# Two neighbouring loads swapped in the first q phase, and a group of small matmuls moved three column tiles later

## The chip, the cores and the metric

The kernel runs on one core of one Trainium2 chip. The metric is the time of one execution on the device in microseconds (us), lower is better. Each kernel is run several times, alternating with the kernel before on the same chip; "span" is the time from the first to the last instruction in the profiled execution, which is about 1.8 us less than the device time of that execution.

## The reference

One transformer block: layer norm with a conditioned scale and shift ("adaLN"), linear attention, and a gated feed-forward part.

```python
def reference(A_x, A_wqkv, A_wo, B_x, B_w_gate, B_w_up, B_w_down, c, w_mod):
    x = A_x                                         # (1, 2048, 1024), bf16
    mod = (_silu(c) @ w_mod).reshape(c.shape[0], 6, 1, -1)
    sa, ca, ga, sb, cb, gb = ...                    # shift, scale, gate; 1024 each   [cut]
    h = _layernorm(x, axis=-1) * (1 + ca) + sa
    x = x + ga * _A_ref(h, A_wqkv, A_wo)            # q, k, v = h @ wqkv ...
    h = _layernorm(x, axis=-1) * (1 + cb) + sb
    x = x + gb * _B_ref(h, B_w_gate, B_w_up, B_w_down)
    return x
```

The change touches only the first step: the scale `ca` (columns 1024-2047 of `w_mod`) and the q part of `h @ wqkv` for the first 512 of 2048 rows. That is the first 30 us of 830.

## The kernel before

The first phase is a race between the load queue and TensorE. All loads of the phase are put on one queue, in this order:

```python
        ca_load(0)          # w_mod columns of the scale, 0-511, 1 MB     -> WCA
        wq_load(0, 2)       # q weights, k-tiles 0 and 1, 512 KB          -> WQK
        ca_load(1)          # scale columns 512-1023, 1 MB
        wq_load(2, 2)       # q weights, k-tiles 2 and 3, 512 KB
        wq_load(4, 2)
        sa_load(1)          # shift columns 512-1023, 1 MB                -> WSA
        wq_load(6)
        wq_load(7)
        sa_load(0)          # shift columns 0-511, 1 MB
        # ... x tiles of the next chunk, k weights ...   [cut]
```

`mod_sc` multiplies those columns by silu(c), one output column per matmul; `q_part` adds some k-tiles to the q product of one column tile `nt`; there are seven column tiles in flight, one PSUM bank each.

```python
        def mod_sc(w, c0, ms):                       # 8 matmuls of ONE column for each m
            for m in ms:
                for kt in range(NDT):
                    P.pe("matmul", out=PS[:, 0, c0 + m:c0 + m + 1], lhsT=w[:, kt, m * 128:(m + 1) * 128],
                         rhs=SILUC[:, kt:kt + 1], ...)           # [cut]

        def q_part(nt, bank, dts):                   # one matmul of 512 columns for each dt
            for dt in dts:
                P.pe("matmul", out=PS[:, bank, :], lhsT=WQK[:, dt, nt * 128:(nt + 1) * 128],
                     rhs=HT[:, 0, dt, :], start=(dt == 0), stop=(dt == 7))

        def q_phase_chunk0(side):
            # ... k-tiles 0 and 1 of the seven column tiles: 14 matmuls   [cut]
            mod_sc(WCA, 8, range(4, 8))              # 32 one-column products: needs ca_load(1)
            fin_ca(4, 4)
            for dt in (4, 5):
                h0_scale_only(dt)                    # VectorE makes k-tiles 4, 5 of the activations
            for nt in range(7):
                q_part(nt, qb[nt], (2, 3))           # 14 matmuls: needs wq_load(2, 2)
            act_stats(4)
            for nt in range(7):
                if nt == 4:
                    mod_sc(WSA, 0, range(6, 8))      # 16 one-column products: needs sa_load(1)
                    # ...   [cut]
                q_part(nt, qb[nt], (4, 5))
            # ... k-tiles 6 and 7, mixed with the other shift columns   [cut]
```

Dependencies are found by the program itself: each instruction waits on semaphores for the last writer or readers of what it touches.

## Time and profile before

| | before |
|---|---|
| device time, median of 3 | 831.19 us (831.15 to 832.09) |
| span of the profiled execution | 829.4 us |
| TensorE matmul busy | 824.0 us, 99% |
| weight-load busy | 378.4 us, 46% |
| VectorE / ScalarE busy | 38% / 24% |

The chain of work that ended last, in order of time (start us, length us, what), is one TensorE piece from 8.76 us to the end. Ahead of it stand the load of the third x tile and the operations of VectorE (DVE) and ScalarE (ACT) that make this tile ready:

```profile
...
1.71 4.21 DMA xres<-in_A_x_dram
...
5.94 1.29 DVE stats L176 x2
...
7.47 1.23 ACT xres L176
8.71 0.05 issue
8.76 818.08 PE ps L176 x4069
826.83 0.02 issue
826.86 0.29 DVE xres L176
```

The waits of TensorE (waited for: us in total, times, longest us) name no weight and no scale column:

```profile
...
PE ps L176 <- DMA cs<-in_c_dram: 2.2, 1, 2.2
PE ps L176 <- ACT xres L176: 0.4, 1, 0.4
PE ps L176 <- DVE e L176: 0.2, 1, 0.2
```

The timeline of TensorE in the first q phase (start us, us to the end of the group, operation, count, and in brackets the idle time before it). `siluc,wca` are scale-column products, `ht,wqk` are q products, `siluc,wsa` are shift-column products:

```profile
...
12.43 3.18 PE L176 MATMUL ps<-ht,wqk 128*128 128x512 bf16 x14
15.45 0.94 PE L176 MATMUL ps<-siluc,wca 128*128 128x1 bf16 x32
16.25 4.91 PE L176 MATMUL ps<-ht,wqk 128*128 128x512 bf16 x22
21.00 0.54 PE L176 MATMUL ps<-siluc,wsa 128*128 128x1 bf16 x16
...
```

Read the *starts*, not the busy times. 22 q products from 16.25 to 21.00 are (21.00 - 16.25) / 22 = 0.216 us each. The Trainium skill ("TensorE: Matmul & The Clock Gate", "Wait — 56ns, not 53.3ns?") gives 215.7 ns from start to start for 512 columns on a warm array; this trace agrees, so no wait hides among them. One record, however, lasts 0.38 us (mean of the q-product group), longer than the step to the next one. So a wait shorter than about 0.16 us leaves no idle time at all in this view, and a longer one looks 0.16 us shorter than it is. The view also leaves out idle times under 0.15 us, so that waits up to about 0.3 us can be missing from it.

The same stretch for weight loads shows when each load is first *wanted*: 0.21 us ahead of the matmul for the column products, which follow q products (15.24 and 15.45, 20.79 and 21.00), and 0.02 us ahead for the q products, which follow column products (16.23 and 16.25):

```profile
...
15.24 1.06 PEld L176 LDWEIGHTS ps<-siluc,wca 128*128 128x128 bf16 x32
16.23 4.44 PEld L176 LDWEIGHTS ps<-ht,wqk 128*128 128x128 bf16 x22
20.79 0.66 PEld L176 LDWEIGHTS ps<-siluc,wsa 128*128 128x128 bf16 x16
...
```

And these loads *landed* (all 16 shares of each) at 14.80 (scale columns 512-1023), 16.17 (q weights 2-3) and 20.46 (shift columns 512-1023); the shift columns 0-511 landed at 24.83 and were wanted at 25.11. The margins are 0.44, 0.06, 0.33 and 0.28 us, counted to the weight load. (No view shows the shares; they are read from the semaphore updates in the kept traces.)

### The profile page before, as it was taken

Reading aid. Unit: us, or ns where it says so; the run is one execution under the profiler, and the core shown is the slowest. Engines: PE = TensorE matmul, PEld = TensorE weight load, DVE = VectorE, ACT = ScalarE, POOL = GpSimd, SP = SyncE. Lnnn points to the kernel's source line nnn. Section 1 sums busy time; section 2 is a strip of 40 time slices with the busy share of each in tenths; the row PEclk is TensorE's granted clock in tenths of the full one; section 3 lists DMA queues with packets and bytes.
Section 4 is the critical chain, followed back from the end, with each engine's and each line's share of the span. In section 5 each row is a group of like instructions: output and inputs, shape, how many; then the busy total and the mean of one; then the engine's idle time right before and its main releaser. Section 6 shows DMA issues by size and latency. Waiting matters only on the chain.

```text
span 829.4 us, 10017 instructions
## 1 busy us (share of the span) xinstructions
PE 824.0 (99%) x4083; PEld 378.4 (46%) x4083; DVE 312.0 (38%) x665; ACT 197.6 (24%) x336; POOL 39.8 (5%) x57
## 2 busy tenths in 40 slices
PE   8999999999999999999999999999999999999998
PEld 4544444454444444444444444444444444444444
DVE  5797986756955521121221111122111111221111
ACT  4757641323242111011111101111110111111011
POOL 1010000000130000030000003000000300000000
PEclk9999999999999999999999999999999999999999
DMA  9969655928397996700455570045557004553000
GB/s 320 288 151 229 149 159 172 202 102 304 60 258 225 259 267 174 192 25 14 128 150 155 150 188 28 15 126 153 153 153 187 26 18 125 154 151 86 0 26 26
DMA packets 199245, 119.28 MB, mean 144 GB/s; under 512 B 57880, under 2 KB 182944, under 8 KB 199200
## 3 DMA queue, kind: packets, MB, share of 16 engines
q1 hardware_dynamic: 199184, 118.65, 52.7%
q8 instruction: 32, 0.52, 0.3%
q14 instruction: 13, 0.11, 0.0%
q10 hardware_dynamic: 16, 0.00, 0.0%
HBM read 100.67 MB, written 4.33 MB: 127 GB/s over the span
## 4 chain that ended last, share of the span: by engine, by line
PE 99%; DMA 1%; DVE 0%; ACT 0%; SPq 0%; issue 0%
PE ps L176 99%; DMA xres<-in_A_x_dram 1%; DVE stats L176 0%; ACT xres L176 0%; SPq L176 0%; DVE xres L176 0%; DVE mv L176 0%; DVE nmr L176 0%
## 5 line engine op out<-in xcount | busy, mean ns | idle before, releaser
L176 PE MATMUL ps<-h2t,gug 128*128 128x512 bf16 x896 | 211.7, 379 | 0.0
L176 PE MATMUL ps<-h2t,guu 128*128 128x512 bf16 x896 | 211.7, 379 | 0.0
L176 DVE TENSOR_TENSOR at<-sg,ps 128x512 bf16<-128x512 bf16 x112 | 77.1, 688 | 282.7 <-PE ps L176 281.1
L176 ACT ACTIVATE sg<-ps 128x512 bf16<-128x512 f32 x112 | 66.9, 597 | 309.7 <-PE ps L176 309.7
L176 PEld LDWEIGHTS ps<-h2t,guu 128*128 128x128 bf16 x896 | 87.5, 98 | 105.8
L176 PEld LDWEIGHTS ps<-h2t,gug 128*128 128x128 bf16 x896 | 87.4, 98 | 105.7
L176 PE MATMUL ps<-wd_a,at 128*128 128x512 bf16 (+1 forms) x512 | 112.4, 378 | 0.0
L176 PE MATMUL ps<-ht,wqk 128*128 128x512 bf16 x512 | 111.7, 379 | 0.0
L176 PE MATMUL ps<-wd_b,at 128*128 128x512 bf16 (+1 forms) x384 | 85.0, 378 | 0.0
L176 PEld LDWEIGHTS ps<-wd_a,at 128*128 128x128 bf16 x512 | 50.0, 98 | 59.8
L176 DVE TENSOR_TENSOR ut<-att,gb_b 128x512 bf16<-128x512 bf16 (+1 forms) x32 | 13.8, 430 | 167.5 <-ACT att L176 167.5
L176 PEld LDWEIGHTS ps<-ht,wqk 128*128 128x128 bf16 x512 | 49.4, 98 | 58.8
L176 ACT ACTIVATE att<-ps 128x512 bf16<-128x512 f32 (+1 forms) x32 | 17.4, 591 | 182.1 <-PE ps L176 182.1
L176 PEld LDWEIGHTS ps<-wd_b,at 128*128 128x128 bf16 x384 | 37.5, 98 | 44.7
L176 PE MATMUL ps<-pk,xres 128*128 128x512 bf16 x256 | 56.5, 379 | 0.0
L176 PE MATMUL ps<-mw,pqt 128*128 128x512 bf16 x256 | 56.3, 379 | 0.0
L176 POOL TENSOR_SCALAR h2t<-h2t,modcol 128x512 bf16<-128x512 bf16 x32 | 26.4, 841 | 383.0 <-DMA h2t<-xn 383.0
L176 ACT ACTIVATE e<-ps 128x512 bf16<-128x512 f32 x56 | 33.1, 603 | 31.7 <-PE ps L176 20.5
L176 PEld LDWEIGHTS ps<-mw,pqt 128*128 128x128 bf16 x256 | 24.8, 98 | 30.3 <-DVE xres L176 0.4
L176 PEld LDWEIGHTS ps<-pk,xres 128*128 128x128 bf16 x256 | 24.8, 98 | 30.0 <-issue 0.4
L176 ACT ACTIVATE junk<-xres 128x1024 bf16<-128x1024 bf16 x24 | 25.4, 1058 | 35.1 <-DVE xres L176 34.9
L176 DVE SCALAR_TENSOR_TENSOR xres<-ps,xres 128x512 bf16<-128x512 f32 x32 | 21.4, 689 | 12.3 <-PE ps L176 11.7
(107 smaller groups left out, 346.0 us busy)
## 6 DMA issues: line engine op xcount, KB each, us to landing
gug<-in_B_w_gate_dram SPq DMA_DIRECT2D x56, 512.0 KB, 3.9
guu<-in_B_w_up_dram SPq DMA_DIRECT2D x56, 512.0 KB, 5.2
xres<-in_A_x_dram SPq DMA_DIRECT2D x20, 256.0 KB, 7.8
rb<-recip_den SPq DMA_DIRECT2D x8, 512.0 KB, 11.5
stgx<-in_w_mod_dram SPq DMA_DIRECT2D x2, 2048.0 KB, 7.8
wd_a<-in_B_w_down_dram SPq DMA_DIRECT2D x4, 1024.0 KB, 7.8
out_dram<-xres SPq DMA_DIRECT2D x31, 128.0 KB, 1.7
xres<-in_A_x_dram SPq DMA_DIRECT2D x3, 1024.0 KB, 14.0
```

Of the source, the lines that this page charges most:

```text
L176: return getattr(e, method)(**kw)
```

## The change

Intent: the q weights of k-tiles 2 and 3 are the load with the least time in hand. They change places with the larger load ahead of them, and to make up for that, the products of the load that is now later go three column tiles (six matmuls) later. No work is added or removed.

```diff
         ca_load(0)
         wq_load(0, 2)
+        wq_load(2, 2)
         ca_load(1)
-        wq_load(2, 2)
         wq_load(4, 2)
@@
-            mod_sc(WCA, 8, range(4, 8))
-            fin_ca(4, 4)
-            for dt in (4, 5):
-                h0_scale_only(dt)
             for nt in range(7):
+                if nt == 3:
+                    mod_sc(WCA, 8, range(4, 8))
+                    fin_ca(4, 4)
+                    for dt in (4, 5):
+                        h0_scale_only(dt)
                 q_part(nt, qb[nt], (2, 3))
```

## The prediction

> **What bounds the kernel.** TensorE, without a pause. The chain of waits that ended last is one unbroken TensorE piece from 8.76 us to 826.83 us (818.08 of 829.4 us). The list of TensorE's waits holds three, 2.8 us in all, every one before 8.8 us; none is for a q weight or a scale column. In the timeline of the first q phase, 22 matmuls of 512 columns start at 16.25 and the next group at 21.00: 0.216 us each. The Trainium skill ("TensorE: Matmul & The Clock Gate", "Wait — 56ns, not 53.3ns?") gives 215.7 ns from start to start on a warm array; the trace agrees, so no stall hides inside the "busy" time. The 32 scale-column products take 15.45 to 16.25, 0.80 us.
>
> **What the change does.** It adds and removes no work; it moves two things.
> 1. Load order. The 1 MB of scale columns 512-1023 and the 512 KB of q weights 2-3 swap. The DMA engines are saturated here (about 360 GB/s from 5 to 30 us in the windows). Landings, from issue plus time to landing: scale columns 14.80, q weights 16.17. First uses, from the weight-load rows of the timeline: 15.24 and 16.23; margins 0.44 and only 0.06 us. The Trainium skill ("DMA: Bandwidth & Descriptors", "Queues, rings and completion order") says that each DMA engine takes descriptors in ring order, and the landings here follow the issue order. So after the swap q weights 2-3 should land at about 13.2 (the first q-weight load's 11.80 plus 1.37, the step between two such loads, 16.17 to 17.55), the scale columns at about 16.2, later loads as before.
> 2. Product order. The k-tile 2-3 products of three column tiles (6 x 0.216 = 1.29 us) go ahead of the scale-column products. They start at 15.24 with 2.0 us in hand; the scale columns are then needed at 16.53, margin about 0.36 us. VectorE makes k-tiles 4-5 ready 1.04 us after the column products end (before: 16.26 to 17.30), thus at about 18.6; their first use stays at about 19.2. No new wait.
>
> **On the critical path.** All the matmuls are, but their sum does not change and no wait before them exists to be removed. The tightest of these margins grows from 0.06 to about 0.3 us (shift columns: landed 20.46, used 20.79, unchanged). That is insurance: it pays only in executions where a load is late. The profiled run (831.22 us) equals the median (831.19), so unprofiled runs hardly stall either. I take 0.05 us for occasional lateness.
>
> **Predicted: 831.1 us, 8 in 10 from 830.5 to 831.9.** Faster by over 2%: 0.005; within 2%: 0.99; slower by over 2%: 0.005.
>
> **What would show it.** Right: one TensorE piece of about 818 us from about 8.8; no wait on a weight or scale load; six q products from about 15.45, the 32 column products at about 16.74; q weights 2-3 landing near 13.2, scale columns near 16.2; everything from 21.0 at its old time. Wrong: a start-to-start over 0.216 us at the scale-column products (columns late) or at the first k-tile 4 product near 19.3 (VectorE late); or a gain over 0.3 us, which would mean stalls in the unprofiled runs of before.
>
> **What would make it wrong.** The 0.06 us margin fails often in unprofiled runs or on another chip, so the swap gains some tenths; or the scale columns land over 0.36 us later than computed; or the start (8.76 us) or the array's warm-up differs between runs by more than these tenths (832.09 was seen among three).

## More of the kernel before

All runs quoted here are at a granted clock of 1.0. The runs of experiments 1 and 2 come from one chip (5), those of 3 and 4 from a second (15), those of 5 from a third (8); for the first result no chip is on record. Profiles of different experiments can thus differ by the chip, too.

## The result

| | before | after |
|---|---|---|
| device time, median (lowest to highest) | 831.21 us (830.95 to 832.09, 6 runs) | 830.94 us (830.53 to 831.58, 6 runs) |
| span of the profiled execution | 829.4 us | 829.4 us |
| ratio after/before | | 0.9996, 95% interval 0.9983 to 1.0009: same |

A ratio here is the mean time of one kernel's fast runs over the mean of the other's in the same rounds, so it is not quite the ratio of the medians in the table.

The total looks like nothing happened. The profile after does not. The chain now has a detour through a load:

```profile
...
7.79 13.09 DMA wsa<-in_w_mod_dram
20.88 0.05 issue
20.93 805.88 PE ps L176 x3932
826.81 0.02 issue
826.83 0.29 DVE xres L176
```

The waits of TensorE have a new entry:

```profile
...
PE ps L176 <- DMA cs<-in_c_dram: 2.2, 1, 2.2
PE ps L176 <- ACT xres L176: 0.9, 1, 0.9
PE ps L176 <- DMA wsa<-in_w_mod_dram: 0.2, 1, 0.2
PE ps L176 <- DVE e L176: 0.2, 1, 0.2
```

The timeline of TensorE in the same phase:

```profile
...
11.97 4.48 PE L176 MATMUL ps<-ht,wqk 128*128 128x512 bf16 x20
16.29 0.94 PE L176 MATMUL ps<-siluc,wca 128*128 128x1 bf16 x32
17.09 3.61 PE L176 MATMUL ps<-ht,wqk 128*128 128x512 bf16 x16
20.93 0.55 PE L176 MATMUL ps<-siluc,wsa 128*128 128x1 bf16 x16 [0.23 <-DMA wsa<-in_w_mod_dram]
...
```

Its weight loads:

```profile
...
16.07 1.06 PEld L176 LDWEIGHTS ps<-siluc,wca 128*128 128x128 bf16 x32
17.07 3.14 PEld L176 LDWEIGHTS ps<-ht,wqk 128*128 128x128 bf16 x16
20.93 0.47 PEld L176 LDWEIGHTS ps<-siluc,wsa 128*128 128x128 bf16 x16 [0.71 <-DMA wsa<-in_w_mod_dram]
...
```

Three things are to be read here.

First, the move itself is as designed: 14 + 6 = 20 q products, then the 32 column products, then 16 q products. The columns are done at 17.09, VectorE has k-tiles 4 and 5 ready at 18.15, 1.06 us later, and their first use follows at 17.09 + 8 x 0.216 = 18.82 without a wait.

Second, one and the same wait at the shift columns is told three ways: 0.23 us in the TensorE row, 0.71 us in the weight-load row, and by the starts 20.93 - 17.09 - 16 x 0.216 = 0.39 us. Only the last is what it cost. The first is too small because a matmul's modelled end lies after the next one's usual start: the Trainium skill ("Perfetto Trace Analysis", "Tensor Engine Instruction (MATMUL, LD_WEIGHTS)") says that the end is estimated, and records of 0.38 us at steps of 0.216 us agree. The second is too large because the weight row is idle about 0.12 us before each load anyway, and the wanted load runs ahead of the matmul: it came 0.59 us late, the matmul 0.39 us. So the margins at column products (0.44, 0.33 and 0.28 us) understate by 0.15 to 0.2 us how late a load may come before it costs anything; the 0.06 us at q weights 2-3 does not.

Third, the chain's shares changed a lot (TensorE 99% before; 97% after, with DMA 2% and the issuing queue 1%) because of a 0.39 us wait. A chain is followed back through what released a wait, so a wait of any length turns it off TensorE, here for the whole 13.09 us in which that load stood in the queue. The shares don't price the wait.

TensorE started the q products 0.46 us earlier than in the profile before (11.97 against 12.43) and lost 0.39 us of it at the shift columns. The change did not touch that start: the loads and operations that TensorE needs up to 12 us are the same ones, in the same order, in both kernels. So is the 0.46 us luck, and the 0.39 us a price of the change? The first has an answer in the kept traces. In the profile before, the third x tile landed at 5.92 us and TensorE's first transpose of the phase started at 8.76; in the profile after, 5.45 and 8.29. In eleven of the twelve profiles of this document the second follows the first by 2.84 us (3.07 in late_room). That tile is issued ahead of everything that the change moves, and its landing varies from 5.06 to 6.13 us; why, the traces don't tell. On the second: the shift columns keep their place in the queue and in TensorE's order, 36 q products and 32 column products after q start (8.57 us, 12.43 to 21.00 in the profile before). With this start and this landing the kernel before would have waited as long. Whether the swap itself can delay that landing takes experiments.

### The profile page after: what moved, and what is told of

Read it like the earlier page. It is cut to its first block, busy times and chain, and to the rows that moved or that the text cites. A ratio compares the mean times of both kernels' runs of the same rounds, so it can differ in the third digit from the quotient of the medians.

```text
span 829.4 us, 10017 instructions
## 1 busy us (share of the span) xinstructions
PE 823.2 (99%) x4083; PEld 378.8 (46%) x4083; DVE 312.6 (38%) x665; ACT 197.5 (24%) x336; POOL 39.9 (5%) x57
## 4 chain that ended last, share of the span: by engine, by line
PE 97%; DMA 2%; SPq 1%; issue 0%; DVE 0%
PE ps L176 97%; DMA wsa<-in_w_mod_dram 2%; SPq L176 1%; DVE xres L176 0%
## 6 DMA issues: line engine op xcount, KB each, us to landing
xres<-in_A_x_dram SPq DMA_DIRECT2D x3, 1024.0 KB, 14.1
```

## The experiments

Two theories were put up.

- **Theory S (sum).** The time is TensorE's start plus a fixed sum of matmuls plus whatever waits remain on loads. A wait is paid once, in full.
- **Theory F (floor of the loads).** In the first phase TensorE runs into the load stream. What it wins in front it gives back at the next load, so waits trade against each other and the end does not move.

Twelve profiles are read in the same way. *q start* is the start of the first q product (of the filler, where there is one); *waits* are the sum, after that point, of the excess of start-to-start over 0.216 us per q product (and 0.80 us for 32 column products) at those places where a load is waited for; *rest* is span minus q start minus waits, and minus 0.86 us of filler where there is one. Waits ahead of q start, on x tiles and on the first scale columns, are inside q start (in after_again 0.59 us at the latter). A wait of 0.03 us in after and in late_after, at shift columns 0-511, is left in the rest.

| profile | q start | waits on loads, us (where) | span | rest |
|---|---|---|---|---|
| before | 12.43 | 0 | 829.44 | 817.01 |
| after | 11.97 | 0.39 (shift 512-1023) | 829.42 | 817.06 |
| before_again | 12.65 | 0 | 829.62 | 816.97 |
| after_again | 12.83 | 0 | 829.81 | 816.98 |
| loads_only | 12.23 | 0.46 (scale 512-1023) | 829.67 | 816.98 |
| products_only | 12.17 | 0.31 (q weights 2-3) | 829.55 | 817.07 |
| pad4_before | 12.24 | 0 | 830.11 | 817.01 |
| pad4_after | 12.55 | 0 | 830.39 | 816.98 |
| late_before | 12.09 | 0.85 (scale) + 0.54 (q 2-3) | 830.47 | 816.99 |
| late_after | 12.30 | 1.02 (scale) + 0.13 (shift) | 830.50 | 817.05 |
| room | 12.18 | 0 | 829.18 | 817.00 |
| late_room | 11.92 | 0.26 (scale) + 0.53 + 0.46 (shift) | 830.15 | 816.98 |

### 1. The kernels again: `before_again` and `after_again`

No edit; the same two kernels on another occasion, five runs each.

> The kernel before, once more, unchanged: the noise floor and a second profile. Theory S (TensorE's sum is the floor; the waits of the first phase are zero or a few tenths): ratio 1.000 within 0.0005, chain of TensorE without a wait from about 8.8 us. Theory F (in the first phase TensorE runs into the DMA stream, so waits there come and go with the landing of the slowest share of a load): this profile shows another pattern, a wait of 0.1 to 0.9 us at q weights 2-3 or at the shift columns, and TensorE's start of the q phase and that wait trade against each other, so that the shift-column products still start at 20.9 to 21.5.

> The changed kernel, unchanged: a second profile. Theory S: ratio to the kernel before 0.9995 to 1.0000. Theory F: also near 1, because the wait at the shift columns (0.23 us in the first profile of the changed kernel) takes what the front won; the shift-column products start at 20.7 to 21.3, right at the landing of their load, in this profile too.

Measured: before_again 831.40 us median (830.89 to 831.71), ratio 1.0001 (0.9988 to 1.0013). After_again 831.57 us (831.20 to 832.32), ratio 1.0005 (0.9992 to 1.0017), against 830.99 us for the kernel before. So the changed kernel was 0.27 us ahead in the first series and 0.58 us behind in this one, by medians, both inside the intervals: no difference. (Theory S had expected a ratio of 0.9995 to 1.0000 for after_again; 1.0005 is above that, inside the noise.)

The profile of after_again has no wait at the shift columns. It has one that the change can't have made, at the scale columns 0-511, the first load of the phase:

```profile
...
11.12 0.55 PE L176 MATMUL ps<-siluc,wca 128*128 128x1 bf16 x16 [0.44 <-DMA wca<-in_w_mod_dram]
...
12.83 4.48 PE L176 MATMUL ps<-ht,wqk 128*128 128x512 bf16 x20
17.14 0.94 PE L176 MATMUL ps<-siluc,wca 128*128 128x1 bf16 x32
17.95 3.61 PE L176 MATMUL ps<-ht,wqk 128*128 128x512 bf16 x16
21.40 0.54 PE L176 MATMUL ps<-siluc,wsa 128*128 128x1 bf16 x16
...
```

Eight transposes start at 10.08, and where no load is waited for the products after them follow 0.45 us later; here they start at 11.12 instead of 10.53, 0.59 us late, and from there everything is late by that much. The margins that the prediction had read from a single profile are thus not constants. Here are the landings of two loads, by shares (a load is done when the last of its 16 shares has landed):

```
us: first / eighth / last of 16 shares      q weights 2-3            shift columns 512-1023
before                                      14.22 / 14.47 / 16.17    18.52 / 18.77 / 20.46
before_again                                13.93 / 14.24 / 15.76    18.26 / 18.54 / 20.20
after                                       11.15 / 11.57 / 11.97    18.43 / 18.86 / 20.88
after_again                                 11.11 / 11.71 / 13.79    18.66 / 19.05 / 21.13
```

With the same load order, the first half of the shares lands within about 0.5 us from one execution to the next; the last share lags by 0.8 to 2.7 us behind the first, and by different amounts. Neither the chip nor the loads ahead explain this: for q weights 0-1, up to which all kernels have the same queue, the lag was 1.83, 2.72, 1.61 and 1.44 us in the four profiles of experiments 1 and 2, all from one chip. Within one execution, however, the lag is not drawn anew at each load. In these four profiles and in before and after it stays the same within 0.1 us over the five loads that follow the x tiles, and can take another value, steady again, from shift columns 512-1023 on: 1.9 and 1.9 us in before, 0.8 and 2.45 us in after. So the wait in after came about by an x tile that was early by 0.46 us together with a lag that grew by 1.6 us. The swap moves the first share of q weights 2-3 by about 2.9 us (14.1 to 11.1), which is the other load's share of the stream; what the last share does on top is not explained by these runs. Theory F's expectation for this pair (a wait at one of the two loads in before_again, shift columns starting right at their landing in after_again) failed: no wait, and starts at 21.21 with a landing at 20.20 and at 21.40 with one at 21.13. (The range given for the first start, 20.9 to 21.5, did hold, but at TensorE's own pace.) The second was close: the first weight load followed the landing by 0.05 us (21.18), but the products kept their pace.

### 2. Half of the change at a time: `loads_only` and `products_only`

```diff
 loads_only: the loads swapped, the products where they were
-        ca_load(1)
         wq_load(2, 2)
+        ca_load(1)

 products_only: the products moved (as in the change), the loads in the old order
```

> Only the load order is swapped; the column products stay ahead of all q products of k-tiles 2-3. Scale columns 512-1023 land at 15.0 to 16.2 and are wanted at 14.8 to 15.24. Theory S: a wait of 0.2 to 0.9 us at the column products and the same amount more time (ratio 1.0003 to 1.001). Theory F: a wait there, too, but the wait at the shift columns shrinks by as much, so the total is within 0.2 us of the kernel before.

> Only the products are moved; loads as in the kernel before. The first q products of k-tile 2 want their weights at 14.8 to 15.24, and these land at 15.0 to 16.2. Theory S: a wait of 0.2 to 0.9 us at the first k-tile-2 product, and as much more time. Theory F: the wait is there but is paid back at the shift columns; total within 0.2 us of the kernel before.

Measured: loads_only 831.47 us (831.12 to 831.98), ratio 1.0003 (0.999 to 1.0016); products_only 831.33 us (830.79 to 831.79), ratio 1.0002 (0.9989 to 1.0016). The device times can't tell either from the kernel before. The profiles can. In loads_only TensorE comes to the scale columns too early:

```profile
...
12.23 3.18 PE L176 MATMUL ps<-ht,wqk 128*128 128x512 bf16 x14
15.71 0.95 PE L176 MATMUL ps<-siluc,wca 128*128 128x1 bf16 x32 [0.30 <-DMA wca<-in_w_mod_dram]
16.52 4.91 PE L176 MATMUL ps<-ht,wqk 128*128 128x512 bf16 x22
21.27 0.54 PE L176 MATMUL ps<-siluc,wsa 128*128 128x1 bf16 x16
...
```

15.71 - 12.23 - 14 x 0.216 = 0.46 us of wait, and none after it: it is carried to the end. In products_only TensorE comes to q weights 2-3 too early, and here the TensorE row shows no idle time at all:

```profile
...
12.17 4.79 PE L176 MATMUL ps<-ht,wqk 128*128 128x512 bf16 x20
16.80 0.94 PE L176 MATMUL ps<-siluc,wca 128*128 128x1 bf16 x32
17.60 3.61 PE L176 MATMUL ps<-ht,wqk 128*128 128x512 bf16 x16
21.05 0.54 PE L176 MATMUL ps<-siluc,wsa 128*128 128x1 bf16 x16
...
```

The 20 q products take 16.80 - 12.17 = 4.63 us instead of 20 x 0.216 = 4.32; one step, at the first product of k-tile 2, is 0.31 us too long. In the list of waits of the weight loads it does appear:

```profile
...
PEld ps L176 <- DMA wqk<-in_A_wqkv_dram: 0.6, 1, 0.6
...
```

So each half by itself opens a wait of 0.3 to 0.5 us where its load is the later of two, in one profile each, and the two halves of the change belong together. Both waits were paid, as theory S says, but q started 0.2 to 0.3 us earlier than in the profile before, so the spans hardly differ.

### 3. Filler ahead of the phase: `pad4_before` and `pad4_after`

```diff
             fin_ca(2, 2)
             for dt in (2, 3):
                 h0_first(dt, "dve")
+            warm(4, bank=3)        # four idle matmuls of 512 columns: 0.86 us
             for nts, dts in (...):
```

If the loads set the pace, TensorE has time to spare in front of them, and a filler is free; if TensorE's sum sets it, the filler costs its length.

> The kernel before with four idle 512-column matmuls (0.86 us) put ahead of the first q product; nothing else. Theory S (TensorE's sum plus whatever waits remain): both profiles of the kernel before had no wait on a load, so all of it is paid: +0.86 us, ratio about 1.0010, and no wait on a load in the profile. Theory F (the loads pace the first phase): most of it is absorbed in front of the loads, under +0.4 us, ratio under 1.0005.

> The changed kernel with the same four matmuls. Theory S: +0.86 us less the waits that this hides (0 to 0.39 us at the shift columns in the two profiles so far), so +0.5 to +0.86 us, ratio 1.0006 to 1.0010; no wait at the shift columns. Theory F: under +0.4 us.

Measured: pad4_before 831.83 us (831.75 to 832.41), ratio 1.0007 (0.9994 to 1.0021); pad4_after 832.20 us (831.95 to 833.18), ratio 1.0012 (1.0000 to 1.0025); the kernel before 831.28 us. The intervals are wide: +0.55 and +0.92 us by medians, between theory F's limit of +0.4 and the full 0.86 plus noise. The profiles settle it. Neither shows a wait on a load after the filler, and with 0.86 us taken off both have the same rest as the others, 817.01 and 816.98. All of the filler is in the span (pad4_after's ratio, 1.0012, even lies above the 1.0006 to 1.0010 that theory S gave, inside the noise). With loads on time, TensorE's sum is what counts.

### 4. Late on purpose: `late_before` and `late_after`

The swap is insurance, so it should be looked at where it has to pay. Two tiles of x (512 KB) are loaded ahead of the disputed pair instead of after the phase; all later loads of the phase move back by that.

```diff
         wq_load(0, 2)
+        for j in range(2):
+            P.dma("x1_%d" % j, XRES[:, 4 + j, :], xv[:, 4 + j, :])
         ca_load(1)              # late_after: wq_load(2, 2) first, products three tiles later
         wq_load(2, 2)
 ...
         sa_load(0)
-        for j in range(2):
-            P.dma("x1_%d" % j, XRES[:, 4 + j, :], xv[:, 4 + j, :])
```

> Lateness on purpose: two x tiles (512 KB, 1.37 us of the load stream) go ahead of the scale columns and q weights 2-3, which thus land 1.37 us later, and all loads after them up to the shift columns of tiles 0-511; order and products of the kernel before. Theory S with margins of 0.44 and 0.06 to 0.69 us: waits of 0.7 to 0.95 us at the column products and 0 to 0.4 us at the q products after them, 0.7 to 1.3 us in sum, and as much more time (ratio 1.0008 to 1.0016).

> The same lateness in the changed kernel. No wait at q weights 2-3 (2 us in hand); 0.3 to 1.0 us at the column products; then at the shift columns (margin about 0.3 us before, load 1.37 us later) the rest up to about 1.0 us. Sum 0.6 to 1.1 us; so of the insurance that the change buys no more than about 0.3 us shows, because the next margin, which it did not touch, is the limit. Ratio 1.0006 to 1.0014, not clear of the kernel above.

Measured: late_before 832.64 us (831.83 to 833.00), ratio 1.0014 (1.0001 to 1.0026); late_after 832.38 us (831.66 to 832.83), ratio 1.0012 (0.9999 to 1.0025). The order of the two is as expected, but the runs overlap. In late_before both disputed loads are waited for:

```profile
...
12.09 3.18 PE L176 MATMUL ps<-ht,wqk 128*128 128x512 bf16 x14
15.96 0.95 PE L176 MATMUL ps<-siluc,wca 128*128 128x1 bf16 x32 [0.69 <-DMA wca<-in_w_mod_dram]
17.30 4.92 PE L176 MATMUL ps<-ht,wqk 128*128 128x512 bf16 x22 [0.39 <-DMA wqk<-in_A_wqkv_dram]
22.05 0.54 PE L176 MATMUL ps<-siluc,wsa 128*128 128x1 bf16 x16
...
```

In late_after the wait at q weights 2-3 is gone and two others stand in its place, a larger one at the scale columns and a small one (0.13 us, shown by the step to 22.03 alone) at the shift columns:

```profile
...
17.64 0.95 PE L176 MATMUL ps<-siluc,wca 128*128 128x1 bf16 x32 [0.86 <-DMA wca<-in_w_mod_dram]
18.45 3.61 PE L176 MATMUL ps<-ht,wqk 128*128 128x512 bf16 x16
22.03 0.55 PE L176 MATMUL ps<-siluc,wsa 128*128 128x1 bf16 x16
...
```

Waits: 0.85 + 0.54 = 1.39 us against 1.02 + 0.13 = 1.15 us, so 0.24 us less with the change, both sums a little above what was expected (0.7 to 1.3 and 0.6 to 1.1 us). But the q phase happened to start 0.21 us later, which shortens the waits by as much, and the shift-column products start at 22.05 and 22.03, the same. Taken by itself this is what theory F says.

It is not a fair pair, though, because the load streams of the two executions differ. The later load of the disputed pair landed at 17.25 us in late_before (q weights) and at 17.59 in late_after (scale columns), the shift columns at 21.66 and 21.99: 0.34 and 0.33 us later with the change. At each of these waits TensorE went on 0.05 us after the landing. An estimate from these numbers puts late_after on the landings of late_before: scale-column products at 17.30, shift columns wanted at 17.30 + 0.80 + 16 x 0.216 = 21.56, started at 21.71 because their load landed at 21.66. That is 0.34 us ahead of 22.05, so the swap would have paid about 0.3 us, and would have been stopped by the next load in the queue, as was expected. One pair of profiles doesn't show it, and the device times (832.64 and 832.38 us) overlap.

With the loads put back by 1.37 us of the stream, an earlier start of the q phase would only have lengthened the first wait in both kernels. In late_after the insurance ends at the next load in the queue, which the change left as it was.

### 5. More room at two loads: `room` and `late_room`

If the next margin is the limit, widening it too should show. On top of the change, the scale-column products go four tiles late instead of three, and the shift-column products for k-tiles 6-7 one tile later.

```diff
-                if nt == 3:
+                if nt == 4:
                     mod_sc(WCA, 8, range(4, 8))
 ...
-                if nt == 4:
+                if nt == 5:
                     mod_sc(WSA, 0, range(6, 8))
```

> The changed kernel with both margins widened: the scale-column products four column tiles late instead of three, and the shift-column products for k-tiles 6-7 one column tile later (0.43 us each). Theory S: no wait on scale columns 512-1023 or shift columns in the profile unless a load is 0.7 us late; the time is that of both kernels, ratio 0.999 to 1.0005, since there is hardly a wait to remove (0 to 0.4 us per profile so far). q start plus waits on loads plus about 817.0 us gives the span again. A wait of VectorE's making at the first k-tile-4 or k-tile-6 product would show as a matmul step over 0.216 us there; expected none (0.25 and 0.15 us in hand).

> The same widened margins under the lateness of 512 KB. Theory S: the waits fall by 0.43 us against the kernel with the three-tile delay and the same lateness (1.15 us in its profile): 0.3 to 0.8 us in sum, ratio 1.0004 to 1.001. If the loads paced the phase instead (theory F), the sum of q start and waits would stay at 13.4 to 13.5 us, as in the two late kernels; theory S wants about 13.0.

Measured: room 831.28 us (830.95 to 832.06), ratio 1.0004 (0.9990 to 1.0017), no wait on any load in the profile, as expected. Late_room 832.47 us (831.95 to 832.94), ratio 1.0016 (1.0003 to 1.0028): no gain over late_after in device time. Its span is 0.3 us shorter than those of the two late kernels, but the profiled run was also the fastest of its five. Its waits were expected to fall to 0.3 to 0.8 us in sum. They are 0.26 + 0.53 + 0.46 = 1.25 us. The first did fall (1.02 to 0.26), and then the shift columns were waited for twice:

```profile
...
21.71 0.55 PE L176 MATMUL ps<-siluc,wsa 128*128 128x1 bf16 x16 [0.35 <-DMA wsa<-in_w_mod_dram]
...
24.32 1.46 PE L176 MATMUL ps<-ht,wqk 128*128 128x512 bf16 x6
26.07 0.95 PE L176 MATMUL ps<-siluc,wsa 128*128 128x1 bf16 x32 [0.30 <-DMA wsa<-in_w_mod_dram]
```

The second of these, at 26.07, is the *last* large load of the phase (shift columns 0-511, landed 26.03), whose products had not been given more room. q start plus waits is 13.17 us, where the two late kernels have 13.48 and 13.45, theory S wanted 13.0 and theory F 13.4 to 13.5. Half a miss: the widened margins passed the lateness on to the load behind, as in experiment 4. (In these two profiles one matmul record in about fifty is missing, so q start is read from the weight-load rows there, and a missing record is counted as a step.)

No version beats both kernels by anything that these runs can show.

## Why the prediction was right

It was right in what decides: 831.1 us was predicted, 830.94 us measured, in a range of 830.5 to 831.9. That the number came within 0.2 us is partly luck: the same kernel had a median of 831.57 us on the next occasion. What the runs support is that there was nothing to gain.

- *TensorE bounds the kernel, and the change does not alter its sum.* Shown. Twelve profiles give a rest of 816.97 to 817.07 us once q start and waits are taken off, over all the orders of the phase that were tried.
- *No wait to remove.* Shown for q weights 2-3: two profiles of the kernel before have none there, and the q products run at 0.216 us. The products_only kernel, with the old load order, shows that a wait does come up at just this load as soon as its products are wanted earlier.
- *The two halves compensate.* Shown, with one profile of each half: each alone opens a wait (0.46 and 0.31 us), both together none at either load.
- *VectorE is ready in time.* Shown: 1.06 us from the last column product, use 0.67 us after that, no long step.
- *Insurance of at most the difference to the next margin.* Not shown. Under deliberate lateness the waits fell by 0.24 us, but 0.21 us of that is the later q start; TensorE reached the shift columns at the same time, and the device times overlap. On equal landings an estimate (experiment 4) gives 0.34 us, near the predicted difference between margins of 0.06 and 0.3 us. A gain in an execution that is late by chance was not seen.

Three steps of it were wrong in size or stated too firmly.

- *"q weights 2-3 should land at about 13.2 [...], the scale columns at about 16.2".* They landed at 11.97 and 14.96 in one profile, and at 13.79 and 16.80 in the other. The step that was added, 1.37 us from one such load to the next, held (1.36 and 1.35 us). What failed was its base, the landing of q weights 0-1 at 11.80 us in one profile: it was 10.61 and 12.43 us in the two others, because the lag of the last share varies by more than a microsecond from execution to execution.
- *The margin of 0.33 us at the shift columns ("landed 20.46, used 20.79, unchanged"), and "no wait on a weight or scale load".* In the first profile after there was a wait of 0.39 us there: TensorE was 0.46 us earlier and the last share 0.42 us later. So the one TensorE piece of 818 us from 8.8 us, which was to show that the prediction is right, did not come: it had 805.88 us, from 20.93. A margin read from one profile has the run-to-run spread of both ends in it.
- *"I take 0.05 us for occasional lateness."* That can't be confirmed or denied here. q start alone varies from 11.92 to 12.83 us over the twelve profiles, by some 18 times the claimed gain.

So with the loads on time TensorE's sum decides, as theory S says (experiment 3). With the loads put back by 1.37 us, the landing of the last load that is waited for, plus the products behind it, decides, and q start does not (experiments 4 and 5). That the end then doesn't move whatever the order, as theory F has it, is not shown. Both kernels lie near the border: in their four profiles one wait on a load of more than 0.03 us came after q start, the 0.39 us.

Open: which executions of the kernel before, if any, stall at q weights 2-3, and how often. Only the profiled ones can be looked into, and neither of those of the unedited kernel did. Which of the 16 shares lags, and why, the trace doesn't tell; nor why the x tile lands early or late.

## What to carry to other kernels

Before reordering loads, find out whether the engine that bounds the kernel waits for them: compare start-to-start of its instructions with the full rate, since idle time and the chain's shares can under- or overstate a wait. A change that only widens a margin is worth nothing while the margin holds, and when it fails, probably no more than the next margin behind it in the same queue (estimated here, not shown by the times); so list all margins first, take them from several profiles, and move a load and its use together. To tell a few tenths of a microsecond among runs that spread over one, split each profiled span into start, waits and rest: the rest here repeated to 0.1 us where device times did not to 1 us.

## What the Trainium skill lacked or had wrong

- "DMA: Bandwidth & Descriptors", table of "Latency and other measured facts": it calls some DMA engines usually slower and, as a best guess, takes that for particular to transfers issued by GpSimd. Here all bulk loads are issued by SyncE, and the last of the 16 shares of a load still land 0.8 to 2.7 us after the first, by varying amounts (shift columns: 18.43 first, 19.11 for the fifteenth, 20.88 for the last). Whether these are the same engines, the trace doesn't say.
- The same page, "Queues, rings and completion order": that each DMA engine takes descriptors in ring order agrees with the first shares here (the swap moved q weights 2-3 from 14.2 to 11.1 us). What it lacks for planning is the size of the last share's lag: 0.8 to 2.7 us behind the first, different by over a microsecond from execution to execution, but steady within 0.1 us over the five loads behind the x tiles in the nine profiles whose queue was not put back.
- "Perfetto Trace Analysis", "Tensor Engine Instruction (MATMUL, LD_WEIGHTS)": it says that the end of a matmul is estimated, but not what that does to waits. Here it hides about 0.16 us of every one: 0.39 us shows as 0.23, 0.46 as 0.30, and 0.31 as none, since what is left of it is too short to be listed.
- "TensorE: Matmul & The Clock Gate", "Wait — 56ns, not 53.3ns?": agrees. 512 columns step by 0.216 us, and one-column products by 0.80 / 32 = 0.025 us, which is the floor that it states. The idle matmuls at the start step by about 0.43 us up to 7.7 us, its rate for a cold array, while the profile's granted clock reads 1.00 for the first 5 us. The page's own caveat, that clock events in traces have been seen to be unreliable, agrees; go by the steps.
